# Transformer block with local attention and a gated MLP: the Q/K/V weight loads move from ScalarE's DMA queue to SyncE's, and the list scheduler's load rate and priorities are set anew

## The chip, the cores and the metric

The kernel runs on one core of a Trainium2 chip. A core has five engines with an instruction stream each: TensorE (PE, matrix products), VectorE (DVE), ScalarE (ACT), GpSimd (POOL) and SyncE (SP, here only the issue of DMA transfers). The metric is the device time of one execution in microseconds (us), the median of several executions; lower is better.

## The reference

One sequence of 2048 tokens of width 448 passes through two residual branches. A is attention with 16 heads of width 28, in which each token sees itself and seven earlier tokens at distances 2, 4, ..., 14. B is a gated MLP in which one matrix `w_sp` of 2048 x 2048 mixes the tokens.

```python
def _A_ref(x, wqkv, wo):                      # D = 448, H = 16, Dh = 28, W, dil = 8, 2
    q, k, v = split_heads(x @ wqkv)
    idx = pos[:, None] - (jnp.arange(W) * dil)[None, :]
    mask = idx >= 0
    logits = einsum('bhsd,bhswd->bhsw', q, k[..., idx, :]) * Dh ** -0.5
    attn = softmax(where(mask, logits, -1e9))
    return einsum('bhsw,bhswd->bhsd', attn, v[..., idx, :]) -> [B, S, D] @ wo
def _B_ref(x, w_in, w_sp, b_sp, w_out):       # F = 1792, Fh = 896
    z = gelu(x @ w_in)
    z1, z2 = z[..., :Fh], layernorm(z[..., Fh:])
    g = einsum('ts,bsf->btf', w_sp, z2) + b_sp[None, :, None]
    return (z1 * g) @ w_out
h   = x + _A_ref(layernorm(x), wqkv, wo)
out = h + _B_ref(layernorm(h), w_in, w_sp, b_sp, w_out)
```

(shortened; the gathers and transposes of the original are written as index expressions)

## The kernel before

The kernel describes its work as tasks: each has the engines on which it may run with an assumed duration, what it reads and writes, and a priority. On the host, when the program is built, a list scheduler places all tasks in assumed time. What the chip gets is fixed: one instruction order for each engine, with semaphore waits for the dependencies. Numbers such as the assumed DMA rate or a priority therefore act on the chip only through the order (and through the choice of engine where a task has several).

```python
DMA_GBS = 280.0                                # assumed load rate, KB per us
P = dict(ln_s=0.02, ln_o=-13.63, qk_s=3.12, qk_o=-20.82, qk_g=-4.37, v=11.1, ve=6.53, lg=-12.86, ...)   # priorities
...
    if t.dma:                                  # in schedule(): when a load is assumed to have landed
        dma_free = max(dma_free, s + 1.5) + t.dma_us
        t.end = max(t.end + DMA_US, dma_free + 0.5)
...
def dma(fn, kb, ..., on="sp"):                 # a transfer; `on` is the engine that issues it
    t = G.add([(on, 0.5)], [fn], reads, writes, ..., dma_us=kb / DMA_GBS)
    t.dma = True
```

The tokens lie in 16 blocks of 128. The start of the kernel, in the order of the text:

```python
for m in range(4):
    load_x(m, 1)                                               # x, block by block: SP
chunks(wv, A_wqkv[:, 2 * D:], 458, r_stv, -99.968, on="act")   # V weights, two transfers: ACT
halves(stg, r_stqk, A_wqkv[:, 0:D], A_wqkv[:, D:2 * D], 401, -99.965, on="act")   # Q and K weights: ACT
load_x(4, 4)                                                   # blocks 4..7: SP
load_x(8, 8)                                                   # blocks 8..15: SP
for u in range(7):                                             # Q/K weights, padded to 32 per head: stg -> wqk
    G.add([("act", ...), ("pool", 0.62), ("dve", 0.33)], [copy], reads=r_stqk, writes=[r_wqk[u]], prio=-6.2)
for i in range(NWARM):                                         # fill matmuls for gaps of PE, result unused
    G.add([("pe", ...)], [matmul(bank(wb, 512), ident, warm)], ..., prio=900)
```

The fill matmuls (line 561) have the lowest priority; the scheduler drops them once the assumed time passes 28 us. The two layer norms (LN1 on x, LN2 on h) go block by block through DVE and GpSimd:

```python
def layernorm(m, i, prio):
    ... bn_stats, bn_aggr (DVE); rstd (POOL); tring = (x - mean) * rstd (DVE)
    if i:                                  # LN2: transposed by DMA into xB, halves swapped by DMA into xS, per pair of blocks
        dma_t(xB[m] <- tring)
        if m % 2: dma(xS[LO] <- xB[HI]); dma(xS[HI] <- xB[LO])
        return
    transpose on PE, evicted by ACT or DVE into xT (in the space of wsp0)
    if m < P["npt"]:   copies of the swapped halves into xU, xU3 by DVE or ACT      # blocks 0..3
    elif m % 4 == 3:   three DMA transfers for blocks m-3..m into xU, xU3           # blocks 4..15
```

Then follow, per group of 512 tokens, four qk pairs (14 matmuls 128x512 of K = 64 each, line 626, reading `xT` and `xU`), and in 18 attention blocks of 114 tokens: V (line 634), logits LG (667), exp (ACT, 676), mask (DVE, 683), AV (688), normalisation (DVE), the transpose OT (700), and y with `wo` (634). LN2 and the two halves of the MLP's input product follow: z2 (line 626, 128x448) and z1 (line 626, 128x512). `w_sp` is read by 64 DMA transposes of 512 columns each (line 467); the first 32 may start once the last V product no longer needs `xT` and the Q/K/V weights, whose space they take. The big product G (line 794) and the output product (812) end the kernel. Other loads are held back with `after`:

```python
chunks(wo_sb[:], A_wo, 458, r_wo, 0.5, after=[ln1[5]])
halves(w2[:], r_w2, B_w_in[:, FH:FH + D], B_w_in[:, FH + D:], 401, 8, after=[ln1[11]])
...                                         # w1 and b_sp: after=[ln1[15]]
```

Of the kernel before, what the change touches and what calls it, by code (L numbers as in the profile page):

```python
# [7 lines left out]
D = 448  # L8
# [90 lines left out]

class Task:  # L100
    __slots__ = ("idx", "alts", "fns", "reads", "writes", "adds", "allocs", "prio", "preds", "succs", "n_wait", "eng",
                 "start", "end", "keep", "table", "mode", "twos", "dma_us", "nb", "dma")

    def __init__(self, idx, alts, fns, reads, writes, adds, allocs, prio, keep, table, mode, twos, dma_us):
        self.idx = idx
        self.alts = alts
        self.fns = fns
        self.reads = reads
        self.writes = writes
        self.adds = adds  # L110
        self.allocs = allocs
        self.prio = prio
        self.keep = keep
        self.table = table
        self.mode = mode
        self.twos = twos
        self.dma_us = dma_us
        self.nb = 0.0
        self.dma = False
        self.preds = set()  # L120
        self.succs = []
        self.eng = None
        self.start = self.end = 0.0
# [4 lines left out]
MODE_US = 0.1  # L128
WIN = {"pe": 0.15, "act": 0.05, "dve": 0.15, "pool": 0.05, "sp": 0.05}
DMA_US = 2.6  # L130
DMA_GBS = 280.0
NSEM = 96


P = dict(ln_s=0.02, ln_o=-13.63, qk_s=3.12, qk_o=-20.82, qk_g=-4.37, v=11.1, ve=6.53, lg=-12.86, ex=-11.31, mk=-12.19,
         av=2.5, nm=-3.3, ot=-5.63, y=8.0, ln2=9.02, z0=58.08, zs=-0.19, zb=8, kz2=1, z1=102.84, kl=2, kq=0, kz=5,
         switch=8.05, npt=4, we=28.0, mc=24.4)


class Graph:  # L140
# [30 lines left out]
    def schedule(self):  # L171
        tasks = self.tasks
        for t in tasks:
            t.n_wait = len(t.preds)
            for p in t.preds:
                tasks[p].succs.append(t.idx)
            for b in t.reads + t.writes + t.adds + t.allocs:
                if isinstance(b, Buf):
                    b.left = b.users
        ready = [t for t in tasks if not t.n_wait]  # L180
        free = {"pe": 0.0, "act": 0.0, "dve": 0.0, "pool": 0.0, "sp": 0.0}
        table = None
        mode = 0
        dma_free = 2.0
        order = []
        dropped = 0
        while ready:
            best = None
            cands = []
            for t in [t for t in ready if t.prio >= 900 and free["pe"] > P["we"]]:  # L190
                ready.remove(t)
                dropped += 1
                for b in {id(b): b for b in t.writes + t.adds + t.allocs}.values():
                    b.left -= 1
                    if not b.left:
                        b.pool.free_at[b.slot] = b.last
            if not ready:
                break
            for t in ready:
                base = t.nb  # L200
                for p in t.preds:
                    q = tasks[p]
                    e = q.end + LAT[q.eng]
                    if e > base:
                        base = e
                ok = True
                for pool in {b.pool for b in t.allocs}:
                    n = sum(1 for b in t.allocs if b.pool is pool)
                    at = pool.when(n, t.keep, t.twos)
                    if at is None:  # L210
                        ok = False
                        break
                    base = max(base, at)
                if not ok:
                    continue
                for e, d in t.alts:
                    s = max(base, free[e])
                    if t.table is not None and e == "act" and table not in (None, t.table):
                        s += TABLE_US
                    if e == "pe" and t.mode != mode:  # L220
                        s += MODE_US
                    cands.append((s, s + d, t, e, d))
            assert cands, "no task can start"
            by_task = {}
            for c in cands:
                k = c[2].idx
                if k not in by_task or c[1] < by_task[k][1]:
                    by_task[k] = c
            first = {}
            for c in by_task.values():  # L230
                if c[3] not in first or c[0] < first[c[3]]:
                    first[c[3]] = c[0]
            eng = min(first, key=lambda e: first[e])
            lim = first[eng] + WIN[eng]
            best = min((c for c in by_task.values() if c[3] == eng and c[0] <= lim), key=lambda c: (c[2].prio + (P["switch"] if c[3] == "pe" and c[2].mode != mode else 0.0), c[2].idx))
            s, e_at, t, eng, d = best
            for pool in {id(b.pool): b.pool for b in t.allocs}.values():
                pool.take([b for b in t.allocs if b.pool is pool], t.twos, s)
            t.eng = eng
            t.start = s  # L240
            t.end = s + d
            free[eng] = s + d
            if t.dma:
                dma_free = max(dma_free, s + 1.5) + t.dma_us
                t.end = max(t.end + DMA_US, dma_free + 0.5)
            if eng == "pe":
                mode = t.mode
            if t.table is not None and eng == "act":
                table = t.table
            for b in {id(b): b for b in t.reads + t.writes + t.adds + t.allocs if isinstance(b, Buf)}.values():  # L250
                b.left -= 1
                b.last = max(b.last, t.end + LAT[eng])
                if not b.left:
                    b.pool.free_at[b.slot] = b.last
            order.append(t)
            ready.remove(t)
            for x in t.succs:
                n = tasks[x]
                n.n_wait -= 1
                if not n.n_wait:  # L260
                    ready.append(n)
        assert len(order) + dropped == len(tasks)
        order.sort(key=lambda t: (t.start, t.idx))
        return order


class Sched:
# [8 lines left out]
        self.ops = {e: [] for e in self.EXEC_ENGS}  # L276
        self.ndma = 0

    def issue(self, exe, dma, fns, reads, writes, adds):
        prod, inc = exe, 1  # L280
        if dma:
            prod, inc = "q%d" % (self.ndma % NSEM), 16
            self.ndma += 1
            if prod not in self.keys:
# [65 lines left out]
def bass_sequential_preLN__sliding_local_dilated__mixer_gmlp__prompt_kernel(  # L350
# [15 lines left out]
    with contextlib.ExitStack() as top:  # L366
# [91 lines left out]
            s = sorted(x.slot for x in b)  # L458
            return psum[:].rearrange("p (b c) -> p b c", c=512)[0:p1, s[i]:s[i + 1] + 1:s[i + 1] - s[i], 0:n]

        def dma(fn, kb, reads=(), writes=(), prio=0.0, after=(), adds=(), allocs=(), on="sp"):
            t = G.add([(on, 0.5)], [fn], reads, writes, adds=adds, allocs=allocs, prio=prio, after=after, dma_us=kb / DMA_GBS)
            t.dma = True
            return t

        def dma_t(dst, src, us, reads=(), writes=(), prio=0.0, adds=()):
            t = G.add([("sp", us)], [lambda e: e.dma_start(dst(), src(), transpose=True)], reads, writes, adds=adds, prio=prio)  # L467
            t.dma = True
            return t

        def pe_us(n, cols):
            return n * (cols / 2400.0 + 0.003)
# [39 lines left out]
        for fn, rd, wr in (  # L512
# [5 lines left out]
        ):  # L518
            G.add([("dve", 0.28)], [fn], rd, wr, prio=P["mc"])

        G.add([("act", 0.3)], [lambda e: e.activation(scr[:, 0:1], scr[:, 1:2], AF.Exp)], reads=[r_scr], writes=[r_scr], prio=-90,
              table="exp")


# [2 lines left out]
                                      X[128 * m:128 * (m + n), :].rearrange("(m p) d -> p m d", p=128)),  # L527
                114 * n, writes=r_x[m:m + n], prio=-100 + m * 0.01)

        def chunks(dst, w, kb, rr, prio, after=(), on="sp"):  # L530
            dma(lambda e: e.dma_start(dst[:, 0:3, :], w[0:384, :].rearrange("(c p) n -> p c n", p=128)), kb * 3 / 4,
                writes=[rr[0]], prio=prio, after=after, on=on)
            dma(lambda e: e.dma_start(dst[LO, 3, :], w[384:D, :]), kb / 8, writes=[rr[1]], prio=prio, after=after, on=on)
            G.add([("dve", 0.3)], [lambda e: e.memset(dst[HI, 3, :], 0.0)], writes=[rr[2]], prio=-98)

        def halves(dst, rr, lo, hi, kb, prio, after=(), on="sp"):
            for i, (ps, src) in enumerate(((LO, lo), (HI, hi))):
                dma(lambda e, ps=ps, src=src: e.dma_start(dst[ps], src.rearrange("(u p) n -> p u n", p=64)), kb, writes=[rr[i]], prio=prio, after=after, on=on)

        for m in range(4):  # L540
            load_x(m, 1)
        chunks(wv, A_wqkv[:, 2 * D:], 458, r_stv, -99.968, on="act")
        halves(stg, r_stqk, A_wqkv[:, 0:D], A_wqkv[:, D:2 * D], 401, -99.965, on="act")
        load_x(4, 4)
        load_x(8, 8)
        def load_wsp(tc, dst, res, prio, guard=()):
# [293 lines left out]
        store_ids = {t.idx for t in stores}  # L840
        store_keys = []
        for t in order:
            key = sch.issue(t.eng, t.dma, t.fns, phys(t.reads), phys(t.writes), phys(t.adds))
            if t.idx in store_ids:
                store_keys.append(key)
        nc.sched_order = order
# [38 lines left out]
```

## Time and profile before

| | |
|---|---|
| time, median of 3 executions | 261.28 us (260.76 to 261.64) |
| span of the profiled execution | 259.9 us |
| TensorE clock granted | 1.00 |
| PE busy | 246.6 us (95%) |
| DVE busy | 154.3 us (59%) |
| ACT busy | 98.5 us (38%) |
| POOL busy | 45.9 us (18%) |
| DMA moved | 22.61 MB, mean 87 GB/s |

How to read the profile: the page gives each engine's busy time, then the span in 40 equal slices with the busy share in tenths. The chain of work that ended last is followed back from the last instruction to what released it, step by step. The timeline lists instructions with start and duration in us, and in brackets how long the engine had been idle before and what ended that. Entries such as SPq or ACTq are instructions of an engine's queue that issue transfers; their duration is that of the issue. PEld is TensorE's weight load. Tiles have the program's names: `early` holds `stg`, `wqk` and `wv`, later the second half of `w_sp`; `wsp` holds `xT`, later the first half of `w_sp`. Matmuls overlap, so a busy PE need not be PE at its peak.

### The profile page before, as it was taken

Reading aid. Unit: us, or ns where it says so; the run is one execution under the profiler, and the core shown is the slowest. Engines: PE = TensorE matmul, PEld = TensorE weight load, DVE = VectorE, ACT = ScalarE, POOL = GpSimd, SP = SyncE. Lnnn points to the kernel's source line nnn. Section 1 sums busy time; section 2 is a strip of 40 time slices with the busy share of each in tenths; the row PEclk is TensorE's granted clock in tenths of the full one; section 3 lists DMA queues with packets and bytes.
Section 4 is the critical chain, followed back from the end, with each engine's and each line's share of the span. In section 5 each row is a group of like instructions: output and inputs, shape, how many; then the busy total and the mean of one; then the engine's idle time right before and its main releaser. Section 6 shows DMA issues by size and latency. Waiting matters only on the chain.

```text
span 259.9 us, 5046 instructions
## 1 busy us (share of the span) xinstructions
PE 246.6 (95%) x2077; PEld 122.5 (47%) x2091; DVE 154.3 (59%) x344; ACT 98.5 (38%) x122; POOL 45.9 (18%) x121
## 2 busy tenths in 40 slices
PE   6699999999999997999899999999999999999995
PEld 2245455554565543554454444544444444544442
DVE  4798928999899999788960008333333333333333
ACT  2367577887998983566563000000000000000000
POOL 5855400023200334343540000000000000000000
PEclk9999999999999999999999999999999999999999
DMA  7910976013420555656546530445354530010002
GB/s 198 299 35 14 226 170 155 4 23 81 102 64 20 85 104 121 109 109 112 114 70 160 124 43 20 99 103 82 93 101 102 83 112 0 20 53 0 0 0 71
DMA packets 58342, 22.61 MB, mean 87 GB/s; under 512 B 48144, under 2 KB 57168, under 8 KB 58320
## 3 DMA queue, kind: packets, MB, share of 16 engines
q1 hardware_dynamic: 56912, 21.09, 37.2%
q10 hardware_dynamic: 1408, 1.20, 1.7%
q8 instruction: 16, 0.26, 0.5%
q14 instruction: 6, 0.05, 0.1%
HBM read 6.49 MB, written 1.84 MB: 32 GB/s over the span
## 4 chain that ended last, share of the span: by engine, by line
PE 83%; ACT 4%; DMA 4%; DVE 3%; issue 2%; SPq 1%; ACTq 1%; DVEq 0%
PE psum L794 37%; PE psum L626 23%; PE psum L634 8%; PE psum L812 8%; DMA early<-in_A_wqkv_dram 3%; ACT z1p L676 2%; PE psum L688 2%; PE psum L561 2%; PE psum L667 1%; PE psum L700 1%; DVE z1p L683 1%; ACT qk L611 1%; DMA xS<-xB 1%; PE psum L589 1%; SPq L467 1%
## 5 line engine op out<-in xcount | busy, mean ns | idle before, releaser
L799 DVE TENSOR_TENSOR qk<-psum,bb 128x512 bf16<-128x512 f32 x28 | 19.3, 690 | 68.8 <-PE psum L794 68.8
L794 PE MATMUL psum<-wsp,z2p 128*128 128x512 bf16 x220 | 48.6, 379 | 0.3 <-issue 0.2
L794 PE MATMUL psum<-early,z2p 128*128 128x512 bf16 x217 | 48.3, 379 | 0.4
L676 ACT ACTIVATE z1p<-psum 128x912 bf16<-128x912 f32 (+2 forms) x36 | 33.6, 934 | 2.3 <-PE psum L667 1.8
L794 PEld LDWEIGHTS psum<-wsp,z2p 128*128 128x128 bf16 x224 | 21.9, 98 | 26.5 <-issue 0.4
L794 PEld LDWEIGHTS psum<-early,z2p 128*128 128x128 bf16 x224 | 22.0, 98 | 26.3
L617 POOL TENSOR_TENSOR rstd<-va,mhalf 128x1 f32<-128x1 f32 x48 | 29.7, 619 | 3.5
L626 PE MATMUL psum<-w,xB 64*128 64x448 bf16 x112 | 23.0, 349 | 3.8 <-DMA xS<-xB 2.0
L615 POOL TENSOR_SCALAR va<-mv 128x1 f32<-128x1 f32 x48 | 11.0, 229 | 85.5 <-DVE mv L571 68.2
L626 PE MATMUL psum<-wsp,early 64*128 64x512 bf16 x112 | 25.7, 377 | 0.1
L611 ACT ACTIVATE qk<-psum 128x1024 bf16<-128x1024 f32 (+1 forms) x24 | 20.7, 864 | 9.9 <-PE psum L626 9.3
L626 PE MATMUL psum<-xU,early 64*128 64x512 bf16 x96 | 23.3, 377 | 0.0
L626 PE MATMUL psum<-w,xS 64*128 64x448 bf16 x112 | 23.1, 350 | 0.0
L764 DVE BATCH_NORM_STATS2 st<-z2p 128x6 f32<-128x448 bf16 x32 | 19.4, 607 | 5.2 <-ACT z2p L760 4.8
L812 PE MATMUL psum<-xS,z1p 128*128 128x448 bf16 x112 | 21.8, 352 | 0.0
L626 PE MATMUL psum<-xB,w 64*128 64x512 bf16 x98 | 21.8, 376 | 0.0
L626 PE MATMUL psum<-xS,w 64*128 64x512 bf16 x98 | 21.8, 376 | 0.0
L569 DVE BATCH_NORM_STATS2 st<-x_tm 128x6 f32<-128x448 bf16 x32 | 19.3, 602 | 2.4 <-DMA x_tm<-in_A_x_dram 2.4
L683 DVE TENSOR_TENSOR z1p<-z1p,maskb 128x1824 bf16<-128x1824 bf16 (+2 forms) x18 | 19.8, 1104 | 1.3 <-ACT z1p L676 0.9
L634 PE MATMUL psum<-early,wsp 128*128 128x448 bf16 (+2 forms) x72 | 16.7, 354 | 2.0 <-ACT wsp L611 1.7
L760 ACT ACTIVATE z2p<-psum 128x896 bf16<-128x896 f32 x16 | 14.5, 917 | 10.0 <-PE psum L626 10.0
L786 ACT ACTIVATE z1p<-psum 128x1024 bf16<-128x1024 f32 x14 | 14.3, 1023 | 7.3 <-PE psum L626 7.3
(70 smaller groups left out, 281.7 us busy)
## 6 DMA issues: line engine op xcount, KB each, us to landing
xS<-xB SPq DMA_DIRECT2D x16, 128.0 KB, 2.4
out_dram<-tring SPq DMA_DIRECT2D x16, 112.0 KB, 1.8
xU<-wsp SPq DMA_DIRECT2D x6, 192.0 KB, 4.6
x_tm<-in_A_x_dram SPq DMA_DIRECT2D x1, 896.0 KB, 10.3
w<-in_B_w_in_dram SPq DMA_DIRECT2D x8, 112.0 KB, 5.0
early<-in_A_wqkv_dram ACTq DMA_DIRECT2D x2, 392.0 KB, 7.5
w<-in_B_w_in_dram SPq DMA_DIRECT2D x2, 392.0 KB, 5.0
xS<-in_B_w_out_dram SPq DMA_DIRECT2D x1, 784.0 KB, 5.2
```

The lines of the kernel that those rows point to most:

```text
L569: G.add([("dve", dve_us(D))], [lambda e: e.bn_stats(st[:, s.slot, 0:6], x_tm[:, m, :])], [r_x[m]], [s], [s], prio=prio)
L611: return e.activation(dst, src, AF.Copy)
L617: G.add([("pool", 0.61)], [lambda e: e.tensor_tensor(rstd[:, k:k + 1], va[:, k:k + 1], mhalf[:, 0:1], ALU.pow)], [r_va[k], r_half], [r_rs[ ...
L626: return [lambda e, j=j, u=u: e.matmul(bank2(b, j, n), ws(j, (LO, HI)[j], u), xs(j, (LO, HI)[j], u), start=(u == 0), stop=(u == 6), tile_p ...
L634: return [lambda e, c=c: e.matmul(bank(b, n, 0, m), ws(ALL, c), xs(ALL, c), start=(c == 0), stop=(c == NCH - 1)) for c in range(NCH)]
L676: lambda e, hh=hh: e.activation(E[0:nk, ev.slot, hh * 4:hh * 4 + 8, 0:nq].rearrange("p (b g) q -> p b g q", b=2), banks(lb, hh, 512, nk).r ...
L683: lambda e: e.tensor_tensor(E[0:nk, ev.slot, :, 0:nq], E[0:nk, ev.slot, :, 0:nq], maskb[0:nk, mi:mi + 1, 0:nq].to_broadcast([nk, NHEAD, nq ...
L760: lambda e, zb=zb, m=m: e.activation(z2p[:, m, :].rearrange("p (b c) -> p b c", b=2), banks(zb, 0, D), AF.Gelu_apprx_tanh)],
L764: lambda e, h=h, m=m, s=s: e.bn_stats(st[:, s.slot, 6 * h:6 * h + 6], z2p[:, m, D * h:D * (h + 1)])],
L794: lambda e, s=s: e.matmul(bank(b, 512), z2p[:, s, fc * 128:(fc + 1) * 128], w[:, s, :], start=(s == 0), stop=(s == NB - 1)) for s in range ...
L799: G.add([("dve", dve_us(512))], [lambda e: e.tensor_tensor(ub[:, u.slot, :], bank(b, 512), bb[:, 512 * tc:512 * (tc + 1)], ALU.add)], [b, ...
L812: lambda e, f=f: e.matmul(bank(b, D), z1p[:, f, 128 * m:128 * m + 128], w_out[:, f, :], start=(f == 0), stop=(f == FC7 - 1)) for f in rang ...
```

## The change

The kernel after holds the later loads back until LN1 has advanced, makes the swapped LN1 copies by DMA from block 4 on, has GpSimd's constants later and puts fill matmuls into TensorE's early gaps. The kernel before has these means as well, as its code shows. What differs is, first, that the four loads of the Q, K and V weights are issued by SP, in line with the x blocks, and no longer by ACT; second, that the scheduler assumes a load rate of 180 instead of 280; third, that the priorities in `P` are another set. The computation, its instructions and their sizes are otherwise the same.

```diff
-DMA_GBS = 280.0
-P = dict(ln_s=0.02, ln_o=-13.63, qk_s=3.12, qk_o=-20.82, qk_g=-4.37, v=11.1, ve=6.53, lg=-12.86, ex=-11.31, mk=-12.19,
-         av=2.5, nm=-3.3, ot=-5.63, y=8.0, ln2=9.02, z0=58.08, zs=-0.19, zb=8, kz2=1, z1=102.84, kl=2, kq=0, kz=5,
-         switch=8.05, npt=4, we=28.0, mc=24.4)
+P = dict(ln_s=0.19, ln_o=4.76, qk_s=2.92, qk_o=-24.0, qk_g=-2.69, v=11.08, ve=5.78, lg=-11.27, ex=-12.44, mk=-11.52,
+         av=1.75, nm=-0.08, ot=-8.55, y=10.16, ln2=8.03, z0=65.95, zs=-1.51, zb=10, kz2=3, z1=89.18, kl=2, kq=2, kz=2,
+         switch=8.15, npt=4, we=28.0, mc=28.85)
...
-            if t.dma:
+            if eng == "sp":
                 dma_free = max(dma_free, s + 1.5) + t.dma_us
...
-        def dma(fn, kb, reads=(), writes=(), prio=0.0, after=(), adds=(), allocs=(), on="sp"):
-            t = G.add([(on, 0.5)], [fn], reads, writes, adds=adds, allocs=allocs, prio=prio, after=after, dma_us=kb / DMA_GBS)
-            t.dma = True
-            return t
+        def dma(fn, kb, reads=(), writes=(), prio=0.0, after=(), adds=(), allocs=()):
+            return G.add([("sp", 0.5)], [fn], reads, writes, adds=adds, allocs=allocs, prio=prio, after=after, dma_us=kb / 180.0)
...
-        G.add([("act", 0.3)], [... AF.Exp)], reads=[r_scr], writes=[r_scr], prio=-90, table="exp")
+        G.add([("act", 0.3)], [... AF.Exp)], reads=[r_scr], writes=[r_scr], prio=-99, table="exp")
...
-        chunks(wv, A_wqkv[:, 2 * D:], 458, r_stv, -99.968, on="act")
-        halves(stg, r_stqk, A_wqkv[:, 0:D], A_wqkv[:, D:2 * D], 401, -99.965, on="act")
+        chunks(wv, A_wqkv[:, 2 * D:], 458, r_stv, -99.968)
+        halves(stg, r_stqk, A_wqkv[:, 0:D], A_wqkv[:, D:2 * D], 401, -99.965)
```

(cut: the parameter `on` and the field `dma` go from the other places too)

More of the change, by code (lines that the diff above doesn't have):

```diff
@@ L101 @@
     __slots__ = ("idx", "alts", "fns", "reads", "writes", "adds", "allocs", "prio", "preds", "succs", "n_wait", "eng",
-                 "start", "end", "keep", "table", "mode", "twos", "dma_us", "nb", "dma")
+                 "start", "end", "keep", "table", "mode", "twos", "dma_us", "nb")
     def __init__(self, idx, alts, fns, reads, writes, adds, allocs, prio, keep, table, mode, twos, dma_us):
@@ L118, in __init__ @@
         self.nb = 0.0
-        self.dma = False
         self.preds = set()
@@ L277, in __init__, with issue @@
         self.ndma = 0
-    def issue(self, exe, dma, fns, reads, writes, adds):
+    def issue(self, exe, fns, reads, writes, adds):
         prod, inc = exe, 1
-        if dma:
+        if exe == "sp":
             prod, inc = "q%d" % (self.ndma % NSEM), 16
@@ L459, in banks @@
             return psum[:].rearrange("p (b c) -> p b c", c=512)[0:p1, s[i]:s[i + 1] + 1:s[i + 1] - s[i], 0:n]
-        def dma(fn, kb, reads=(), writes=(), prio=0.0, after=(), adds=(), allocs=(), on="sp"):
-            t = G.add([(on, 0.5)], [fn], reads, writes, adds=adds, allocs=allocs, prio=prio, after=after, dma_us=kb / DMA_GBS)
-            t.dma = True
-            return t
+        def dma(fn, kb, reads=(), writes=(), prio=0.0, after=(), adds=(), allocs=()):
+            return G.add([("sp", 0.5)], [fn], reads, writes, adds=adds, allocs=allocs, prio=prio, after=after, dma_us=kb / 180.0)
         def dma_t(dst, src, us, reads=(), writes=(), prio=0.0, adds=()):
-            t = G.add([("sp", us)], [lambda e: e.dma_start(dst(), src(), transpose=True)], reads, writes, adds=adds, prio=prio)
-            t.dma = True
-            return t
+            return G.add([("sp", us)], [lambda e: e.dma_start(dst(), src(), transpose=True)], reads, writes, adds=adds, prio=prio)
         def pe_us(n, cols):
@@ L519, in bass_sequential_preLN__sliding_local_dilated__mixer_gmlp__prompt_kernel @@
             G.add([("dve", 0.28)], [fn], rd, wr, prio=P["mc"])
-        G.add([("act", 0.3)], [lambda e: e.activation(scr[:, 0:1], scr[:, 1:2], AF.Exp)], reads=[r_scr], writes=[r_scr], prio=-90,
+        G.add([("act", 0.3)], [lambda e: e.activation(scr[:, 0:1], scr[:, 1:2], AF.Exp)], reads=[r_scr], writes=[r_scr], prio=-99,
               table="exp")
@@ L528, in load_x, with chunks, halves @@
                 114 * n, writes=r_x[m:m + n], prio=-100 + m * 0.01)
-        def chunks(dst, w, kb, rr, prio, after=(), on="sp"):
+        def chunks(dst, w, kb, rr, prio, after=()):
             dma(lambda e: e.dma_start(dst[:, 0:3, :], w[0:384, :].rearrange("(c p) n -> p c n", p=128)), kb * 3 / 4,
-                writes=[rr[0]], prio=prio, after=after, on=on)
-            dma(lambda e: e.dma_start(dst[LO, 3, :], w[384:D, :]), kb / 8, writes=[rr[1]], prio=prio, after=after, on=on)
+                writes=[rr[0]], prio=prio, after=after)
+            dma(lambda e: e.dma_start(dst[LO, 3, :], w[384:D, :]), kb / 8, writes=[rr[1]], prio=prio, after=after)
             G.add([("dve", 0.3)], [lambda e: e.memset(dst[HI, 3, :], 0.0)], writes=[rr[2]], prio=-98)
-        def halves(dst, rr, lo, hi, kb, prio, after=(), on="sp"):
+        def halves(dst, rr, lo, hi, kb, prio, after=()):
             for i, (ps, src) in enumerate(((LO, lo), (HI, hi))):
-                dma(lambda e, ps=ps, src=src: e.dma_start(dst[ps], src.rearrange("(u p) n -> p u n", p=64)), kb, writes=[rr[i]], prio=prio, after=after, on=on)
+                dma(lambda e, ps=ps, src=src: e.dma_start(dst[ps], src.rearrange("(u p) n -> p u n", p=64)), kb, writes=[rr[i]], prio=prio, after=after)
         for m in range(4):
             load_x(m, 1)
-        chunks(wv, A_wqkv[:, 2 * D:], 458, r_stv, -99.968, on="act")
-        halves(stg, r_stqk, A_wqkv[:, 0:D], A_wqkv[:, D:2 * D], 401, -99.965, on="act")
+        chunks(wv, A_wqkv[:, 2 * D:], 458, r_stv, -99.968)
+        halves(stg, r_stqk, A_wqkv[:, 0:D], A_wqkv[:, D:2 * D], 401, -99.965)
         load_x(4, 4)
@@ L842, in bass_sequential_preLN__sliding_local_dilated__mixer_gmlp__prompt_kernel @@
         for t in order:
-            key = sch.issue(t.eng, t.dma, t.fns, phys(t.reads), phys(t.writes), phys(t.adds))
+            key = sch.issue(t.eng, t.fns, phys(t.reads), phys(t.writes), phys(t.adds))
             if t.idx in store_ids:
```

## The prediction

> **What bounds the kernel now.** I read the page first. Its busy table and its 40 slices say that TensorE (PE) is nearly full from about 16 us to the end, and half used before that.
>
> ```profile
> PE 246.6 (95%) x2077; PEld 122.5 (47%) x2091; DVE 154.3 (59%) x344; ACT 98.5 (38%) x122; POOL 45.9 (18%) x121
> ...
> PE   6699999999999997999899999999999999999995
> ...
> DVE  4798928999899999788960008333333333333333
> ```
>
> A slice is 6.5 us. "Busy" is not "useful": 39 of the matmuls are fills (L561, product unused), so the time is PE's useful work plus fills and idle time. The useful work is the same in both kernels; I count what is not useful. Next I read the chain of work that ended last, then the timeline of the first 17 us.
>
> ```profile
> 2.52 8.65 DMA early<-in_A_wqkv_dram
> ...
> 11.25 1.51 ACT early L611 x3
> 12.76 0.49 ACT wsp L611
> ...
> 16.39 6.15 PE psum L626 x56
> ```
> ```profile
> 1.85 1.33 ACTq L538 DMA_DIRECT2D early<-in_A_wqkv_dram  x2
> ...
> 11.25 1.51 ACT L611 ACTIVATE early<-early 128x448 bf16<-128x448 bf16 x3 [2.90 <-DMA early<-in_A_wqkv_dram]
> ...
> 13.30 0.93 PE L634 MATMUL psum<-early,wsp 128*128 128x448 bf16 x4 [1.74 <-ACT wsp L611]
> ```
>
> The columns are start, duration, engine, what; the bracket is idle time before it and its releaser. The Q/K weights (784 KB, `stg`) are issued by ScalarE (ACT) at 1.85 us and land at 11.17. ACT then copies them into `wqk`, and the eviction of LN1 block 2 (`wsp L611`) waits behind those copies, so PE waits 1.74 us and the first four qk pairs start at 16.39. That is the first limit. The second is at the change of phase. For it I read the SyncE (SP) queue and PE from 80 to 130 us.
>
> ```profile
> 82.66 1.16 SPq L467 DMA_TRANSPOSE wsp<-in_B_w_sp_dram  x1
> ...
> 100.14 1.17 SPq L584 DMA_DIRECT2D xS<-xB  x2
> ...
> 125.39 1.17 SPq L584 DMA_DIRECT2D xS<-xB  x2
> ```
> ```profile
> 103.21 0.35 PE L626 MATMUL psum<-w,xB 64*128 64x448 bf16 x1 [1.32 <-DMA xS<-xB]
> ...
> 109.37 0.35 PE L626 MATMUL psum<-w,xB 64*128 64x448 bf16 x1 [0.51 <-issue]
> ```
>
> From 82.66 on the SP queue issues one thing after another (about 1.3 us each). LN2's transposes (`xB`), the half swaps (`xS`) and the w_sp transposes stand in one line. PE stands still four times and goes on at 103.2, 109.4, 118.8 and 128.4 us, each time 3 to 4 us after an `xS` issue (the others are at 105.36 and 115.33). So between 83 and 129 us SP's order sets the pace, although PE's slices read 9.
>
> **What the Trainium skill says.** "DMA: Bandwidth & Descriptors", section "Issuing engines are not separate DMA queues": copies from SP and ACT end on the same 16 DMA engines, and a second issuer saves only issue time. The trace agrees: ACT's issues cost 0.46 to 0.66 us of its own time, while both streams together moved 266 GB/s from 5 to 10 us (windows view). The same page, "Queues, rings and completion order": each DMA engine alternates between the rows that have work, and takes one row's descriptors in order. That fits the trace: the weights issued at 1.85 us beside 1.3 MB of x issued at about 2.5 to 4 took until 11.17, as if they shared the rate. "Perfetto Trace Analysis", "Per-instruction lifecycle": an issue's window does not contain the data's movement. Indeed 1.33 us of issue stand against 8.65 us in the chain.
>
> **The change, part by part.**
>
> 1. *Loads.* The four wqkv loads go from ACT's queue to SP's, behind the first four x blocks and ahead of the other twelve. Six x issues took 3.2 us, so an issue is about 0.43 to 0.7 us; the Q/K halves are issued at about 3.9 to 5.3 us instead of 1.85 to 3.2. But in a single line 448 + 392 + 784 KB stand ahead of their end, not 2.35 MB: 1624 KB at 266 GB/s are 6.1 us, from about 2.3 us, so they land near 8.5 to 9.3. That is 2 us sooner than 11.17. x blocks 4 to 7 (448 KB more, 1.7 us) land at about 10.5 to 11, much as now (DVE took block 4 at 11.46). The last eight go from 13.7 to about 14.5, needed at about 17.
>
> 2. *Priorities and the load rate assumed by the scheduler (280 to 180 KB per us).* Read off the built instruction streams. The DVE stream now normalises block 3 before the weight copies; DVE, ACT and POOL take 3, 2 and 2 of the seven copies instead of 1, 5 and 1. Adding up DVE's list from the first x (3.23) with the trace's durations (statistics 0.59, aggregate 0.18, scaling 0.39, eviction 0.41, half copy 0.29): block 3 is scaled at about 10.5, evicted at 11.3, weight copies end at 12.4, last half copy at 12.7. PE's list then has one V, four fills and the first qk pair at about 13.5, against 16.39: **2.9 us gained**. The three mask constants follow on DVE (0.8 us), so block 4 starts at 13.5 instead of 11.46, but now without stops.
>
> 3. *Second qk group.* It needs the DMA half swaps of blocks 4 to 7. The four pairs end at 19.7, four transposes and evictions at 21.3; three issues and 4.6 us to landing give 26.5, against 29.39 now. PE has then done one AV more (0.4) and three transposes less (0.9): the lead is 2.4. Fills after the first qk are 16 in both.
>
> 4. *26 to 80 us.* Now PE runs five qk pairs in a row, and DVE starves (4.82 us before 37.66). The new order has four, and LN1's last blocks lie beside them. From its list DVE has some 29 us of work left from 41 us to the last V matmul (V17), of 37 us; now it has 34 of 36. So PE should keep its lead, or gain the 0.5 us of small stops: 2.4 to 3.1, say **2.9** at V17.
>
> 5. *Change of phase.* V17 releases the w_sp loads, now at 82.6. From there to the eighth `xS` both SP lists hold nearly the same: now 17 w_sp and 9 `xB`, after 16 and 10. At 1.3 us each that is equal. But only six of the LN2 blocks are transposed before V17, not seven, and the next two scalings stand late in DVE's list (about 4.3 and 10.7 us after V17, where SP wants them at 2.7 and 6.7). SP waits there, and pairs 4 to 6 come 2 to 7 us later relative to V17. Part is made up, since the present line also lost 4 us somewhere (42.7 us from V17's release to the last `xS`, for 38.7 of counted work). I give back **1.2 us**. Afterwards, G and the output product are the same in both.
>
> Sum: −2.9 + 1.2 = −1.7; 261.28 − 1.7 = **259.6 us**.
>
> **Rivals.** (A) *The end is tied to SP, and the whole lead is lost there.* For it: PE's stops at each `xS` now; pair 4 of LN2 comes later than before. Against: SP's line begins at V17, which moves with the lead. It makes 261 to 262. (B) *One line of loads is slower than two.* If a full SP queue delays its issues (the wo issue, seventh in line, took 1.94 us), Q/K weights land at 11 or later and x blocks 4 to 15 after them; DVE's list stalls before block 4. It makes 262 to 264. Against: the data rate was no lower with SP alone (244 GB/s from 30 to 35 us). (C) *DVE and ACT relief gives more.* ACT is 90% busy from 60 to 100 us and chain pieces pass through it; a better order could take up 1 to 2 us more, with no loss at the phase change: 257 to 258. Against: ACT receives four more LN1 evictions (0.6 each).
>
> **Range and chances.** My sums for the new kernel contain no unforeseen stops and so lean to the fast side; each chained estimate is good to about 1 us. With (A) and (B) as one side and (C) as the other, 257.2 to 262.8 should hold it 8 times in 10. A 2% gain needs 256.05, that is 5.2 us, more than the whole lead I find: 4%. A 2% loss needs 266.5, which only (B) at its worst gives: 3%. Within 2%: 93%.
>
> **What would show it.** Step 1: the weights land before 10 us and no ACT issue stands at 0.8. Step 2: the first 128x512 qk matmul at 13 to 14.5 us. Step 3: the second group at 26 to 27.5. Step 4: DVE's idle time from 30 to 40 us falls from 5.5 us to under 3; last V at 79 to 80.5. Step 5: PE idle between V17 and the last z2 rises from about 4 us, with a stop for an `xS` near 95 us. I am wrong if the first qk comes after 15.5, if SP's line takes over 45 us from V17 to its last `xS`, or if new stops of PE between 26 and 80 us sum to more than 2 us.

## The result, and the profile after

The changed kernel takes 259.14 us (258.9 to 259.45), beside 261.41 us (260.76 to 261.64) for the kernel before in the same series: a ratio of 0.9918, with a 95% interval of 0.9897 to 0.9939. That is a gain of 2.1 us, between 1.6 and 2.7; 259.6 us was predicted. In the table, all times are in us.

| | before | after |
|---|---|---|
| span of the profiled execution | 259.9 | 257.2 |
| first qk pair starts | 16.32 | 14.38 |
| second qk group starts | 29.32 | 27.17 |
| V17, the last V product, starts | 81.71 | 79.46 |
| last z2 group starts | 128.37 | 125.65 |
| G starts | 138.91 | 136.18 |

The page of the kernel after, busy table and slices of PE and DVE:

```profile
PE 246.3 (96%) x2076; PEld 122.5 (48%) x2090; DVE 154.6 (60%) x342; ACT 99.0 (38%) x123; POOL 46.4 (18%) x122
...
PE   6999999999998999799899999999999999999995
...
DVE  5898979779999999797860009423342333333333
```

The busy times are those of before within 0.5 us, so no work was saved. Two digits tell of the change: PE's second (6.5 to 13 us) was 6 and is 9, since PE's work before the first qk pair now comes sooner; DVE's sixth (32.5 to 39 us) was 2 and is 7, since DVE no longer starves there. Neither says how much time that brings; for this the timeline is needed. First the start, in the timeline of the kernel after:

```profile
12.03 1.08 POOL L606 COPY early<-early 128x448 bf16<-128x448 bf16 x2
...
12.89 1.04 ACT L605 ACTIVATE early<-early 128x448 bf16<-128x448 bf16 x2
...
13.28 0.65 DVE L606 COPY early<-early 128x448 bf16<-128x448 bf16 x3
...
14.38 0.39 PE L620 MATMUL psum<-wsp,early 64*128 64x512 bf16 x1
```

None of the seven weight copies has a bracket: no engine waits for the Q/K weights any more, where ACT had waited 2.90 us for them. The copies now come when their turn comes, on three engines. In the chain of work that ended last, the entry of the weight transfer (8.65 us before) is gone:

```profile
2.27 4.45 PE psum L555 x10
...
102.56 3.31 DMA xS<-xB
...
122.48 2.40 DMA xS<-xB
```

Its place at the head has been taken by the ten fill matmuls of the start (line 555 here, 561 before). The later part of this chain is what it was: PE goes on when an `xS` has landed. In PE's timeline of the kernel after, these are the stops between 84 and 130 us:

```profile
106.51 0.35 PE L620 MATMUL psum<-w,xB 64*128 64x448 bf16 x1 [1.51 <-DMA xS<-xB]
...
115.95 0.35 PE L620 MATMUL psum<-w,xB 64*128 64x448 bf16 x1 [0.57 <-issue]
...
125.65 0.35 PE L620 MATMUL psum<-w,xB 64*128 64x448 bf16 x1 [0.83 <-DMA xS<-xB]
```

There are three where there were four, and the stop near 95 us that the prediction feared is not among them. From the end of V17 to the last `xS` issue SP took 42.1 us (80.38 to 122.48); before, it took 42.8 (82.63 to 125.39). The line of SP still sets the pace there, and it has kept its length.

**What the first qk pair hangs on.** PE's first lines of two profiles, before and after in this order, differ by something that is no part of the change:

```profile
2.27 3.79 PE L561 MATMUL psum<-z1p,ident 128*128 128x512 bf16 x10 [2.27 <-POOL ident L488]
5.89 0.40 PE L589 MATMUL psum<-ident,tring 128*128 128x128 bf16 x4
```
```profile
2.27 4.45 PE L555 MATMUL psum<-z1p,ident 128*128 128x512 bf16 x10 [2.27 <-POOL ident L482]
6.51 0.45 PE L583 MATMUL psum<-ident,tring 128*128 128x128 bf16 x4
```

Both kernels begin with the same ten fills, and the first transpose (T0, the second line) stands behind them. A fill takes 0.43 us at first and 0.22 later, and the ten took 3.79 to 4.45 us in twelve profiles, under either order. The Trainium skill, "TensorE: Matmul & The Clock Gate", section "What you observe", says that PE's clock rises about 4 us into sustained work and that this instant moves by some 0.5 us from run to run. The traces show such a rise, but with more scatter: the fills turn fast 3.0 us after the first one in the kernel before, and in five of the twelve profiles all ten are slow, for 4.2 us. So T0 starts anywhere from 5.89 to 6.51.

Under the new order this shifts all that follows. The kernel after and three variants that begin like it (e3, e5 and e6 below) have T0 at 6.02 to 6.51, and their first qk pair 7.81 to 8.06 us later. Two of DVE's lines in the kernel after show why: block 0 is scaled by 5.42, but its transpose stands behind the fills until 6.51, and DVE waits for it.

```profile
4.87 0.55 DVE L568 TENSOR_SCALAR tring<-x_tm,mv,rstd 128x448 bf16<-128x448 bf16 x1
...
7.00 0.42 DVE L606 COPY wsp<-psum 128x512 bf16<-128x512 bf16 x1 [0.98 <-PE psum L583]
```

The first limit of the new kernel is thus its own fills, which hold T0 back by 0.6 to 1.1 us in these four profiles; fewer of them were not tried. Under the old order it is the Q/K weights. ACT's copies begin when these land, in the kernel before (the prediction shows the line) as in two variants with its order, first e7, which starts as the kernel before does, then e1, which has the loads on SP:

```profile
11.76 1.51 ACT L615 ACTIVATE early<-early 128x448 bf16<-128x448 bf16 x3 [2.92 <-DMA early<-in_A_wqkv_dram]
```
```profile
10.62 1.51 ACT L611 ACTIVATE early<-early 128x448 bf16<-128x448 bf16 x3 [1.33 <-DMA early<-in_A_wqkv_dram]
```

The first qk pair follows 5.06 to 5.08 us after these copies begin in all three (16.32, 16.82 and 15.70). The two orders thus have no common event from which both could be counted, and I compare the profiles as they stand, with their scatter. The first qk pair comes at 16.32 and 16.82 in the two profiles that start like the kernel before, and at 13.83 to 14.57 in the four that start like the kernel after; V17 at 81.71 and 82.62, and at 78.91 to 79.64. The lead of the kernel after over the kernel before is 1.94 us at the first qk pair and 2.25 at V17; between the means of these profiles it is 2.3 and 2.9.

### The profile page after: what moved, and what is told of

The parts are those of the page before. It is cut to its first block, busy times and chain, and to the rows that moved or that the text cites. A ratio compares the mean times of both kernels' runs of the same rounds, so it can differ in the third digit from the quotient of the medians.

```text
span 257.2 us, 5043 instructions
## 1 busy us (share of the span) xinstructions
PE 246.3 (96%) x2076; PEld 122.5 (48%) x2090; DVE 154.6 (60%) x342; ACT 99.0 (38%) x123; POOL 46.4 (18%) x122
## 4 chain that ended last, share of the span: by engine, by line
PE 84%; ACT 4%; DVE 4%; issue 2%; SPq 2%; DMA 2%; POOL 1%; DVEq 0%; POOLq 0%
PE psum L788 37%; PE psum L620 19%; PE psum L628 8%; PE psum L806 8%; PE psum L555 4%; PE psum L682 2%; SPq L463 2%; DMA xS<-xB 2%; PE psum L661 2%; PE psum L583 2%; ACT z1p L670 1%; PE psum L694 1%; DVE tring L568 1%; ACT qk L605 1%; ACT z2p L754 1%
## 5 line engine op out<-in xcount | busy, mean ns | idle before, releaser
L611 POOL TENSOR_TENSOR rstd<-va,mhalf 128x1 f32<-128x1 f32 x48 | 28.3, 591 | 3.6
L609 POOL TENSOR_SCALAR va<-mv 128x1 f32<-128x1 f32 x48 | 12.3, 256 | 82.8 <-DVE mv L565 64.7
```

Source lines behind the costliest of these rows:

```text
L611: G.add([("pool", 0.61)], [lambda e: e.tensor_tensor(rstd[:, k:k + 1], va[:, k:k + 1], mhalf[:, 0:1], ALU.pow)], [r_va[k], r_half], [r_rs[ ...
```

## The experiments

The ratios are to the kernel before on the same chip. The marks are starts in the profile of each kernel, one profile for each, in us; z2 − V17 is the last z2 group's start minus V17's.

| kernel | T0 | first qk pair | V17 | z2 − V17 | ratio (95%) |
|---|---|---|---|---|---|
| before | 5.89 | 16.32 | 81.71 | 46.7 | 1 |
| after | 6.51 | 14.38 | 79.46 | 46.2 | 0.9918 (0.9897 to 0.9939) |
| e1, before with loads on SP | 6.51 | 15.70 | 81.58 | 45.9 | 0.9988 (0.9959 to 1.0018) |
| e2, after with loads on ACT | 6.51 | 15.64 | 80.72 | 46.2 | 0.9966 (0.9943 to 0.9989) |
| e4, before with an earlier eviction | 6.51 | 15.53 | 81.29 | 46.3 | 0.9975 (0.9959 to 0.9991) |
| e5, after without guard waits | 6.51 | 14.57 | 79.64 | 46.7 | 0.9921 (0.9892 to 0.9951) |
| e8, after with quiet GpSimd | 6.02 | 13.73 | 79.62 | 46.7 | 0.9949 (0.9933 to 0.9965) |
| e9, e8 mended | 6.15 | 14.04 | 79.11 | 47.4 | 0.9947 (0.9926 to 0.9968) |
| e3, after with w_sp behind the last xS | 6.31 | 14.17 | 79.24 | 42.8 | 0.9798 (0.9771 to 0.9826) |
| e6, e3 with guard waits | 6.02 | 13.83 | 78.91 | 43.4 | 1.07 (1.0655 to 1.0746) |
| e7, before with e3's edit | 6.39 | 16.82 | 82.62 | 42.9 | 0.9898 (0.9854 to 0.9942) |
| e10, e9 with e3's edit | 6.00 | 13.70 | 78.77 | 42.8 | 0.9797 (0.9769 to 0.9825) |

### e1 and e2: the two halves of the change alone

e1 is the kernel before, all orders kept; only the four weight loads go to SP, behind the first four x blocks:

```diff
+moved = [t for t in order if t.dma and t.eng == "act"]     # the four wqkv loads
+... eng = "sp", placed behind the fourth SP task
```

> All orders of the kernel before, but its four Q/K/V weight loads are issued by SP, behind the first four x blocks and ahead of the others, as in the kernel after. Theory 1 (the order makes the gain: block 3 of LN1 ahead of the weight copies, copies spread over three engines): first qk pair at 16.2 to 16.6 us, time within 0.5 us of before (261.3). Theory 2 (the shorter line ahead of the Q/K weights makes it): weights land by 9.5 us, first qk at 14 to 15, time 259 to 259.7.

Measured: 261.09 us (260.16 to 263.02), no difference from before that can be seen.

e2 is the kernel after, all orders kept, with the four loads back on ACT's queue:

```diff
+moved = [t for t in order if t.eng == "sp"][4:8]           # the four wqkv loads
+... eng = "act", placed at the start of ACT's stream
```

> All orders of the kernel after, but its four Q/K/V weight loads are issued by ACT at the start, as in the kernel before. Theory 1 (order): first qk pair at 14.4 to 15.2 us (x block 1 then lands about 1 us later and holds DVE up by some 0.5 us), time 259.1 to 259.8. Theory 2 (loads): first qk at 16 or later, time 261 or more.

Measured: 260.29 us (259.89 to 261.3).

In these profiles the queue alone brings the first qk pair 0.62 us forward, the orders alone 0.68, both 1.94. That is more than the sum, though not by much more than the 0.5 us by which starts scatter. The queue acts in two ways. In the old order it is worth the time by which the weights come sooner: ACT's wait for them ends at 10.62 in e1, 0.63 us sooner than in the kernel before. In the new order nobody waits for the weights, and yet the queue brings 1.26 us there (e2, the new orders with the old queue, against the kernel after, with T0 at 6.51 in both). The lines are DVE's statistics, of x blocks 0 and 3 in the kernel after, then of blocks 1 and 3 in e2:

```profile
2.88 0.63 DVE L563 BATCH_NORM_STATS2 st<-x_tm 128x6 f32<-128x448 bf16 x1 [1.49 <-DMA x_tm<-in_A_x_dram]
...
5.43 0.59 DVE L563 BATCH_NORM_STATS2 st<-x_tm 128x6 f32<-128x448 bf16 x1
```
```profile
4.75 0.63 DVE L563 BATCH_NORM_STATS2 st<-x_tm 128x6 f32<-128x448 bf16 x1 [0.82 <-DMA x_tm<-in_A_x_dram]
...
7.73 0.63 DVE L563 BATCH_NORM_STATS2 st<-x_tm 128x6 f32<-128x448 bf16 x1 [1.21 <-DMA x_tm<-in_A_x_dram]
```

With the weights on a second queue DVE waits for x twice more, and the new order, in which DVE takes all four blocks' statistics early, pays for it: block 3 is 2.3 us later. The single x blocks land 2.1 us after their issue in the kernel after (median) and 3.6 in e2. The Trainium skill, "DMA: Bandwidth & Descriptors", section "Queues, rings and completion order", has each DMA engine alternate between rows that have work, and that is how it looks: what the second queue took from x is what SP's single line gives back. The gain of the queue move in the new order is not that the weights come sooner, but that the first x blocks do.

The old order cannot keep what the queue gives. e1 is 0.62 us ahead at the first qk pair and 0.13 at V17. PE's timeline of e1 shows where the rest goes, at the fifth qk pair in a row, where PE does not stop in the kernel before (in e7 it stops for 0.47 us):

```profile
35.48 0.37 PE L626 MATMUL psum<-wsp,early 64*128 64x512 bf16 x1 [0.56 <-DMA z1p<-wsp]
```

The half swaps of blocks 8 to 11 are not there yet. The new order has four pairs and then attention, and no such wait. What e1 and e2 do not separate is the assumed load rate from the priorities: the two were changed together, and which of them makes which part of the new orders is not known.

### e4: the eviction that stood behind the copies

The kernel before; ACT evicts LN1 block 2 before three weight copies, not after them:

```diff
+ev = the ACT task that evicts block 2; the weight copies ahead of it go right behind it
```

> The kernel before, with one thing moved in ACT's order: the eviction of LN1 block 2 stands ahead of the three weight copies, not behind them. Theory 1 in its narrow form (that eviction is what kept PE): PE's third V starts 1.5 us or more earlier, first qk at 15 to 15.6 us, time 260 to 260.7. Rival (the copies themselves end too late, since ACT has five of the seven, and the half copies of block 3 follow): first qk at 16 or later, time within 0.4 us of before.

Measured: 260.56 us (259.71 to 261.69). ACT's timeline of e4 has the eviction 1.3 us sooner (12.67 in the kernel before):

```profile
11.36 0.60 ACT L611 ACTIVATE wsp<-psum 128x512 bf16<-128x512 bf16 x1 [2.31 <-PE psum L589]
```

The first qk pair comes 0.79 us sooner and V17 0.42, after the same fifth pair has waited 0.44 us for its half swaps. The place that the prediction named as the first limit was one: this one moved eviction does two fifths of what the whole change does at the first qk pair. Its bracket names PE, no longer the weights, and T0 was 0.62 us later than in the kernel before, so a part of the effect may be hidden.

### e3, e5, e6, e7: SP's line at the change of phase

e3 is the kernel after. All 16 transposes of the second half of `w_sp`, and the seven of the first half that still stood behind, are issued by SP after the last `xS`; of each half, only the first transpose keeps its waits for the old readers of the space (its guards):

```diff
+late = [first-half transposes behind the last xS] + [second half]
+... placed in SP's order right behind the last xS
+for t in wsp_tasks[tc][1:]:
+    t.writes = t.writes[:1]        # its own part of w_sp; without the guards
```

> The kernel after, with one thing moved in SP's line: the 16 transposes of the second half of w_sp stand behind the last swap xS of LN2 (not between them), and each later w_sp transpose no longer waits for the one before. If SP's line sets the pace at the change of phase: 8 transposes of 1.3 us less ahead of the last swap, the last z2 comes when PE and VectorE allow; PE's idle time between the last V and the last z2 falls from 3.7 us to under 1.5 us and the time to 256 to 257.5. If VectorE (91% busy there) or PE sets it: idle time stays at 3 us or more and the time at 258.5 to 259.5. If G then waits for the second half of w_sp, PE shows a new stop after 150 us.

Measured: 255.77 us (255.25 to 256.18). e5 takes the guards off only, e6 makes the move only.

> The kernel after with its orders, in which only the first of each 16 w_sp transposes of the phase change keeps its waits for the old readers of its space (the others stand behind it in SP's order anyway). Theory (SP's number of issues ahead of the xS sets the phase change, not their waits): 259.1 us +- 0.4, from the release of V17 to the last xS still about 42 us, PE idle there still 3.5 to 4 us. Rival (each guard wait costs SP time, and that is what the kernel with the transposes behind the last xS won): 256 to 257.5 us and under 40 us from V17 to the last xS.

Measured: 259.13 us (258.24 to 259.78), the time of the kernel after. The guard waits cost nothing that can be seen there.

> The kernel after with the w_sp transposes moved behind the last xS, but all their guard waits kept. Theory (position on SP alone): 255.8 us +- 0.4, last xS near 115.4, PE idle from V17 to the last z2 under 1 us. Rival (the waits were the cost): 257.5 to 259 us.

Measured: 279.39 us (278.69 to 280.11), which neither theory had. Up to the last z2 group, e6 does what the move was to do: last `xS` at 116.27, PE's only stop 0.48 us. What comes after is new. SP in e3, then SP and PE in e6:

```profile
115.39 1.16 SPq L582 DMA_DIRECT2D xS<-xB  x2
116.60 10.22 SPq L463 DMA_TRANSPOSE wsp<-in_B_w_sp_dram  x7
126.86 21.31 SPq L463 DMA_TRANSPOSE early<-in_B_w_sp_dram  x16
148.21 0.58 SPq L823 DMA_DIRECT2D xS<-in_B_w_out_dram  x1
```
```profile
117.64 17.18 SPq L463 DMA_TRANSPOSE wsp<-in_B_w_sp_dram  x7
134.87 39.47 SPq L463 DMA_TRANSPOSE early<-in_B_w_sp_dram  x16
174.38 0.58 SPq L823 DMA_DIRECT2D xS<-in_B_w_out_dram  x1
```
```profile
179.18 7.32 PE L810 MATMUL psum<-xS,z1p 128*128 128x448 bf16 x28 [21.35 <-DMA xS<-in_B_w_out_dram]
```

Sixteen transposes take 21.31 us in e3 and 39.47 in e6, 1.33 and 2.47 us each. A guard is declared as something that the transpose writes; so each transpose of a half waits until the one before it has landed. In the kernel after, the two halves and the `xB` take turns, which leaves time for the landing (e5 gains nothing without the guards); put behind each other they do not. `w_out` is issued 26 us later, and PE stands still for 21.35 us. Position is what e3 gained by; dropping the guards is what makes the new position possible.

e7 is the kernel before with the edit of e3:

> The kernel before with the same edit as the fastest kernel so far (w_sp transposes behind the last xS, guards stripped). Theory 1 (the lead at V17, 2.25 us, passes through the phase change whole, and SP's line costs both kernels about 3.3 us): 257.9 us +- 0.4, V17 at 81.7, first G product near 135. Theory 2 (with SP's line gone something else in both kernels sets the end, so that loads and orders no longer matter): 255.8 us, the same as the changed kernel with this edit. Theory 3 (SP's line was worth less in the kernel before): over 259 us.

Measured: 258.38 us (257.73 to 259.86), half a microsecond above the first theory's value, far from the second. Between e7 and e3 stand 1.0% or 2.6 us, and V17 is 3.4 us apart in their profiles. So the lead of loads and orders reaches the end with SP's line (after against before) and without it (e3 against e7), and the edit is worth 2.7 us in the old kernel and 3.1 in the new, with overlapping intervals.

In e3 PE's timeline marks no stop between 83 us and the last z2 group; the windows view (window, its length, then busy time of each engine) has for this stretch:

```profile
80.16:122.05 41.89, 41.12 (x477) 20.46 (x475) 40.10 (x97) 31.47 (x34) 18.08 (x42) 1.00 0.49 103
```

PE is busy 41.12 of 41.89 us, in the kernel after 41.64 of 45.32. SP's line is 6.9 us shorter (35.2 instead of 42.1), but the last z2 group comes only 3.4 us sooner after V17, of which 2.9 are time that PE had stood still. PE is now busy for 98% of the stretch and DVE for 96% (40.10 us), so there is little left to gain by SP.

### e8, e9, e10: VectorE beside GpSimd

In the kernel after, the scaling of block 3 took 0.63 us on DVE where it usually takes 0.39, and a half copy 0.69 instead of 0.29, both beside work of GpSimd:

```profile
10.94 0.63 DVE L568 TENSOR_SCALAR tring<-x_tm,mv,rstd 128x448 bf16<-128x448 bf16 x1
...
12.56 0.69 DVE L606 COPY xU<-wsp 64x384 bf16<-64x384 bf16 x1
```

e8 takes GpSimd's memsets of the exp and OT buffers out of this stretch and gives its two weight copies to ACT and DVE:

```diff
+quiet = memsets of E and otm: placed right before the first exp
+cps[0].eng, cps[1].eng = "act", "dve"      # the two weight copies of GpSimd
```

> The kernel after in which GpSimd is quiet from about 10.5 us to the first qk pair: its memsets for the exp and OT buffers (1.7 us) come later, its two weight copies go to ACT and DVE. Theory (DVE instructions beside a GpSimd instruction wait for the port pair that both share: in the kernel after the scaling of block 3 took 0.63 us instead of 0.39, a half copy 0.69 instead of 0.29): scaling at about 10.9 in 0.39 to 0.45, half copies 0.29, and in spite of one more weight copy on DVE (0.27) the first qk pair at 13.9 to 14.1 instead of 14.38; time 258.6 to 259.1. Rival (the long durations come from elsewhere, such as DMA writes at that time): they stay, first qk at 14.6 or later, time 259.1 to 259.5.

Measured: 259.8 us (258.83 to 260.71). DVE's, then ACT's timeline of e8:

```profile
10.40 0.40 DVE L568 TENSOR_SCALAR tring<-x_tm,mv,rstd 128x448 bf16<-128x448 bf16 x1
...
11.75 0.29 DVE L606 COPY xU<-wsp 64x384 bf16<-64x384 bf16 x1
```
```profile
12.08 1.51 ACT L605 ACTIVATE early<-early 128x448 bf16<-128x448 bf16 x3
...
22.18 1.90 ACT L670 ACTIVATE z1p<-psum 114x912 bf16<-114x912 f32 x2 [0.68 <-POOL z1p L501]
```

The durations are what the theory said, 0.40 and 0.29. The Trainium skill, "SBUF — State Buffer", section "Who interferes with whom", has DVE and GpSimd share a pair of ports that one instruction holds to its end while the other waits; copies and scalings are among those that can. Yet no time is won. ACT's copies now end last (13.59), so the first qk pair comes 7.71 us after T0 instead of 7.87; most of the 0.65 us between the two profiles is T0, 0.49 us sooner with shorter fills. And the memsets, in their new place, hold up the first exp (second ACT line) and the rstd of blocks 8 and 9: V17 is 0.65 us later, counted from T0 (73.60 against 72.95; in e3, e5 and e6 it is 72.89 to 73.13). My choice of their place was bad. e9 puts them behind the rstd of block 7, where GpSimd is idle:

> The kernel after with GpSimd quiet until the first qk pair, as before, but its memsets for the exp and OT buffers now stand behind the rstd of block 7, in a gap of about 3 us, and no longer in front of the rstd of blocks 8 and 9. Theory (the first qk pair came 0.65 us sooner in the run before this and the deferred memsets lost it again): first qk 13.7, second qk group 26.5, V17 78.9, 258.5 us +- 0.3. Rival (something else takes the lead of the first pair away before the second group, the half swaps by DMA for instance): second group at 27.0 or later, 259.1 us or more.

Measured: 259.6 us (259.02 to 259.76). V17 is back at 72.96 after T0, as in the kernel after, and no sooner. The expectation took the 0.65 us for the work of the edit; that was wrong. e10 has this edit and that of e3:

> Both useful edits together: w_sp transposes behind the last xS, and GpSimd quiet until the first qk pair with its memsets behind the rstd of block 7. If the lead at V17 passes to the end: 255.77 - 0.6 = 255.2 us +- 0.3, V17 at about 78.7, first G product at about 131.7. If the lead is lost on the way: 255.8.

Measured: 255.78 us (254.78 to 255.98): the lead is not there, and e3 remains as fast as any.

## Why the prediction was right, and where it was not

The predicted time is 0.5 us above the measured one, and each of the five steps can be held against the traces.

**Step 1, loads: the term was mis-sized, without harm.** The Q/K halves are issued at 3.74 and 4.4 us (3.9 to 5.3 predicted), but land up to 6.6 us after issue, at about 11.0 and not at 8.5 to 9.3. The rate of 266 KB per us was that of two queues; SP's line alone moved 218 from 5 to 10 us. Since the copies come from 12.03 on in the new orders, nobody waits. What the move really gave there, x block 3 taken by DVE at 5.43 instead of 7.73 us (after against e2), was not in the sum; it is what made the DVE list of step 2 hold. So the second queue did more than save issue time: with it the small loads that were needed first landed 3.6 us after their issue, without it 2.1. Rival (B), a slower line of loads, is right on the landing and wrong on the time.

**Step 2, first qk pair: right in its mechanism, too large in size.** 2.9 us were predicted, 1.94 are measured (2.3 between the means). The first qk matmul came at 14.38, not 13.5. DVE's list had no waits in it; the trace has 0.98 us of waiting for T0, which the fills held back, and two instructions 0.24 and 0.40 us longer beside GpSimd. e8 and e9 take the second away, at the price of one more copy each for ACT and DVE, and win nothing; no run takes the first away.

**Step 3, second group: right.** Predicted lead 2.4, measured 2.15.

**Step 4, 26 to 80 us: right.** PE should keep its lead or gain up to 0.5 us; it gained 0.3, from 1.94 at the first qk pair to 2.25 at V17. The 2.9 predicted at V17 has step 2's error in it (between the means it is what was found). DVE's idle time from 30 to 40 us fell from 5.46 to 2.03 us, and PE's longest new stop before 84 us is 0.33 us.

**Step 5, change of phase: this step failed.** It gave back 1.2 us, because two LN2 scalings would stand 4.3 and 10.7 us after V17 and SP would wait for them. In the trace they start 1.1 and 6.8 us after SP's line (80.41), and SP does not wait. Here is the second of them, on SP and on DVE:

```profile
86.26 1.26 SPq L463 DMA_TRANSPOSE early<-in_B_w_sp_dram  x1
87.58 1.25 SPq L463 DMA_TRANSPOSE xB<-tring  x1
```
```profile
87.17 0.39 DVE L568 TENSOR_SCALAR tring<-x_tm,mv,rstd 128x448 bf16<-128x448 bf16 x1
```

Of pairs 4 to 6 only the fourth comes later (its `xS` 11.7 us after the start of SP's line, before 7.4), and PE does not stop for it; the other two come 0.6 us sooner. PE's idle time from V17 to the last z2 group was to rise from about 4 us and fell from 4.0 to 3.7. z2 minus V17 is 45.9 to 46.7 us in the three kernels with the old orders (before, e1, e4) and 46.2 to 47.4 in the five with the new ones (after, e2, e5, e8, e9), 46.3 and 46.6 in the mean: if anything is given back, it is a few tenths of a microsecond, inside the scatter. The second limit was correctly named: e3 shows that SP's line costs about 3 us. It was wrong to think that the new order would lengthen it, and rival (A), that it would swallow the lead, is refuted by e7 and e3 as well.

So the −1.7 on record is near the measured −2.1 (−1.6 to −2.7) partly by luck: a lead that was too large at the first qk pair and a loss that did not happen stand against each other. Without the give-back the sum would be −2.9, outside the measured interval. How much of the lead is lost on the way cannot be told to better than some half a microsecond: the execution profiled of the kernel before was the slowest of its runs (261.64 us), that of the kernel after the fastest (258.9), and their spans are 2.7 us apart. Within that, the gains of e1, e2 and e4 in time (0.3, 0.9 and 0.65 us) are those of their profiles at V17 (0.13, 0.99 and 0.42). Rival (C), 257 to 258, did not come: there was no more relief than the list of step 4 had.

## What to carry to other kernels

Before moving a load to another queue, ask whom it shares the rate with: here, under the new order, a load that nobody waited for any more slowed the small ones that everybody waited for. Where one in-order queue issues both what is needed next and what is needed much later, put the later work behind, and see that it doesn't wait for itself there: with its guards dropped this brought 1.2% on top of the 0.8% of the whole change, with them it cost 7%. And before two profiles are compared, follow the chain in each to what its start hangs on: here the fills in one order and the landing of the weights in the other, and both move by about half a microsecond from profile to profile.

## What was not expected of the hardware

- The same ten fills took 3.79 to 4.45 us from profile to profile, at a granted clock shown as 1.00, and under the new order everything from T0 to V17 moved with them.
- The landing of the Q/K weights moves as well: ACT's wait for them ended at 11.25 us in the kernel before and at 11.76 in e7, which has the same loads.
- A transposing load of `w_sp` took 1.33 us of SP's time when it did not wait and 2.47 us when each waited for the one before it to land (e3 and e6).
- Scaling and copies on DVE took 0.63 and 0.69 us beside GpSimd and 0.40 and 0.29 with GpSimd quiet, while BATCH_NORM_STATS2 took 0.59 to 0.63 in both.
- Mean rates in the first microseconds: two queues 266 KB per us from 5 to 10 us, one queue 218; from 10 to 15 us it was 250 against 332, so the single line moved the same data, but later.
